# A third of four gate quarters computed in its PSUM bank, with a new pacing table, in a spectral mixing and gated feed-forward kernel

## The chip, the cores and the metric

The kernel runs on one core of a Trainium2 chip. The metric is the device time of one execution in microseconds. The kernel before took 1727.75 us (median of three runs, 1726.9 to 1728.06).

A core has five instruction streams that run side by side and meet at semaphores: TensorE (PE, with weight loads listed apart as PEld), VectorE (DVE), ScalarE (ACT), GpSimd (POOL) and SyncE (SP), which here only issues DMA transfers. Matrix products end in PSUM, which this kernel uses as eight banks of 128 x 512 float32. Each stream executes its instructions in the order in which the program lists them.

## The reference

The input `x` has 8192 tokens of 448 channels. Two functions of it are multiplied and added to it:

```
xn  = layernorm(x)
s   = irfft( softshrink( W2 . relu( W1 . rfft(xn) + b1 ) + b2 ) )   # along the 8192 tokens; W1, W2 complex,
                                                                    # block-diagonal, 4 blocks of 112
g   = silu( (gelu(xn @ w_gate) * (xn @ w_up)) @ w_down )            # hidden width 1792
out = x + s * g
```

So `s` is a Fourier filter over the tokens and `g` a gated feed-forward layer, token by token.

## The kernel before

**Precision.** Every matrix product is made of float16 parts. A float32 operand is split into a high and a low half, and three products (high by high, high by low, low by high) are added in PSUM. Large products are moreover cut into 2 x 2 blocks and made with seven block products in place of eight (`PROD`, `PROD2`). That leaves many sums and splits of float32 tiles for VectorE, ScalarE and GpSimd.

**Two passes of the feed-forward part.** The 8192 tokens are cut into 16 chunks of 512. The hidden width is cut into 14 tiles of 128: pass one (`p == 0`) handles eight tiles for all chunks and writes each chunk's partial down-projection to DRAM (`prt`); pass two (`p == 1`) handles the other six tiles and adds the partial. A chunk (`chunk`) is a series of units of two hidden tiles (`unit`). A unit makes its products 1, 5, 6, 4, 2, 3, 7 into one bank of the ring `bx` and two banks of the ring `by`; each ring has two banks. Product 1 goes into the `bx` bank `X`; a ScalarE copy (`seed`, seen in the trace as `by<-bx`) takes it to a `by` bank `Z`; product 5 takes the other `by` bank; product 6 (`a6`) adds to `X` and waits for that copy.

**The down-projection** of a chunk (`down2`) makes four quarters, each 128 x 448 (two token columns by half the channels). The first one, `QS[0]`, is built partly in a `bd` bank and partly in a `by` bank `z`; the second in the `bd` bank that serves on for a later quarter; the last two in `bd` banks. Half of this work stands at the end of the chunk, the other half (`tail`) is taken into the first unit of the next chunk.

**The gate of a quarter in pass two** (`ended2`, lines 1811 to 1864). With `u` half the down-projection, `silu(2u) = u (1 + tanh u)`. Three instructions compute it: scale the bank and add the partial loaded from `prt` (VectorE), tanh (ScalarE), `(tanh + 1) * u` (VectorE). The partial lies in one of four SBUF slots (`PT`, seen in the trace as the tile `left`, since the slots lie in that tile's space); SP loads a new partial as soon as a slot is free. For the last two quarters the sum `u` is written back into the bank itself, the slot is free after the first instruction and the bank after the third. For the first two the sum goes to the slot: the bank is free after the first instruction and the slot after the third. The result `th` is then stored to DRAM (`gsp`) for the first eleven chunks, and for the later ones multiplied with `s` at once.

**The Fourier part** runs between these. Phase 1 (until about 645 us) normalizes `x` and does a first transform; phase 2 (until about 1470 us) does the second transform, the block products, softshrink and the first inverse transform in 64 groups; phase 3 does the last inverse transform, multiplies by the gate, adds `x` and stores.

**What sets the order.** The program is written by a planner, the class `Pace`. Each piece of work is a Python generator; `Pace.run` advances them in the order of planned times and so writes one order for each engine. Planned times come from a cost for every instruction (`cost`), the planned end of what it reads (`ready`), and rings that hand out a bank or slot when its last use is planned to be over (`Ring`, `Slots`). The planner's settings change with planned time by the table `STEPS`, whose entries are a time and five numbers: an allowance for each DMA transfer's landing, the backlog at which an engine counts as busy (not in force after phase 1, where a constant 1.8 us is larger), a factor on every cost but TensorE's, a bias in choosing GpSimd over VectorE, and a factor on the distance between the starts of Fourier chunks, groups or tiles. `Either` picks VectorE or GpSimd for sums of SBUF tiles.

Of the kernel before, what the change touches and what calls it, by code (L numbers as in the profile page):

```python
# [22 lines left out]
NG = 16  # L23
# [16 lines left out]
GROUPS = tuple((j, min(4, 64 - j)) for j in range(1, 64, 4))  # L40
POS = (0, 2, 1, 3)
EPS = 1e-5
STEPS = ((0, 2.75, 0.05, 1.0, 0.0, 1.0), (15, 2.75, 0.05, 1.0, 0.0, 1.0), (25, 2.75, 0.05, 0.96, 0.2, 1.0), (35, 2.75, 0.05, 0.96, 0.2, 1.0), (45, 2.75, 0.05, 1.08, 0.1, 1.0), (55, 2.75, 0.05, 1.08, 0.1, 1.0), (65, 2.75, 0.05, 1.07, 0.0, 1.0), (75, 2.75, 0.05, 1.07, 0.0, 1.0), (87, 2.75, 0.15, 0.98, -0.1, 1.0), (100, 2.75, 0.15, 0.98, -0.1, 1.0), (125, 2.5, 0.15, 1.04, 0.0, 1.0), (150, 2.5, 0.15, 1.04, 0.0, 1.0), (175, 2.5, 0.15, 1.04, 0.2, 1.0), (200, 2.5, 0.15, 1.04, 0.2, 1.0), (225, 3.0, 0.15, 1.08, -0.2, 1.0), (250, 3.0, 0.15, 1.08, -0.2, 1.0), (275, 3.0, 0.15, 1.08, -0.2, 1.0), (300, 3.0, 0.15, 1.08, -0.2, 1.0), (325, 3.0, 0.05, 1.03, -0.2, 1.0), (350, 3.0, 0.05, 1.03, -0.2, 1.0), (375, 3.0, 0.05, 1.03, -0.2, 0.9), (400, 3.0, 0.05, 1.03, -0.2, 0.9), (425, 2.5, 0.15, 1.04, -0.5, 1.06), (450, 2.5, 0.15, 1.04, -0.5, 1.06), (475, 2.5, 0.1, 1.04, 0.0, 1.0), (500, 2.5, 0.1, 1.04, 0.0, 1.0), (525, 2.5, 0.1, 1.04, -0.3, 1.0), (550, 2.5, 0.1, 1.04, -0.3, 1.0), (575, 2.5, 0.1, 1.04, -0.2, 0.94), (600, 2.5, 0.1, 1.04, -0.2, 0.94), (625, 2.5, 0.1, 1.06, -0.2, 0.94), (650, 2.5, 0.1, 1.06, -0.2, 0.94), (675, 2.5, 0.1, 1.03, -0.2, 0.94), (700, 2.5, 0.1, 1.03, -0.2, 0.94), (725, 2.5, 0.1, 1.03, -0.3, 0.94), (750, 2.5, 0.1, 1.03, -0.3, 0.94), (775, 3.0, 0.05, 1.04, -0.5, 1.0), (800, 3.0, 0.05, 1.04, -0.5, 1.0), (825, 2.5, 0.05, 1.02, -0.5, 1.0), (850, 2.5, 0.05, 1.02, -0.5, 1.0), (875, 2.5, 0.05, 1.05, -0.5, 1.0), (900, 2.5, 0.05, 1.05, -0.5, 1.0), (925, 2.5, 0.05, 1.05, -0.5, 0.94), (950, 2.5, 0.05, 1.05, -0.5, 0.94), (975, 2.5, 0.05, 1.05, -0.5, 0.94), (1000, 2.5, 0.05, 1.05, -0.5, 0.94), (1025, 4.0, 0.05, 1.05, -0.5, 0.9), (1050, 4.0, 0.05, 1.05, -0.5, 0.9), (1075, 4.0, 0.05, 1.05, -0.5, 0.75), (1100, 4.0, 0.05, 1.05, -0.5, 0.75), (1125, 2.75, 0.05, 1.04, 0.0, 0.94), (1150, 2.75, 0.05, 1.04, 0.0, 0.94), (1175, 1.75, 0.05, 1.075, 0.0, 1.0), (1200, 1.75, 0.05, 1.075, 0.0, 1.0), (1225, 1.75, 0.05, 1.045, -0.5, 0.94), (1250, 1.75, 0.05, 1.045, -0.5, 0.94), (1275, 1.75, 0.05, 1.055, -0.5, 1.0), (1300, 1.75, 0.05, 1.055, -0.5, 1.0), (1325, 1.25, 0.05, 0.995, -0.5, 1.03), (1350, 1.25, 0.05, 0.995, -0.5, 1.03), (1375, 1.25, 0.05, 0.995, -0.5, 0.93), (1400, 1.25, 0.05, 0.995, -0.5, 0.93), (1425, 1.25, 0.05, 0.995, -0.5, 0.93), (1450, 1.25, 0.05, 0.995, -0.5, 0.93), (1475, 1.25, 0.05, 1.025, -0.5, 1.0), (1500, 1.25, 0.05, 1.025, -0.5, 1.0), (1525, 1.25, 0.05, 1.025, -0.5, 1.0), (1550, 1.25, 0.05, 1.025, -0.5, 1.0), (1575, 1.25, 0.05, 1.055, -0.5, 1.06), (1600, 1.25, 0.05, 1.055, -0.5, 1.06), (1625, 1.25, 0.05, 1.055, -0.5, 1.06), (1650, 1.25, 0.05, 1.055, -0.5, 1.06), (1675, 1.25, 0.1, 1.045, -0.5, 1.06), (1700, 1.25, 0.1, 1.045, -0.5, 1.06), (1725, 2.75, 0.05, 0.94, 0.4, 1.0))
QUIET = 200.0
AHEAD = 0.0
FREE = 1.8
# [12 lines left out]
class Pace:  # L59
# [498 lines left out]
def afno_geglu_kernel(ctx, tc, x, gu, raw, wd, mlp, b1, b2, c_m, c_mt, c_small, c_rows, out):  # L558
# [1106 lines left out]
    def add2(p, i, q, bank_):  # L1665

        v = part(bank_, 128, 2, DH)
        if p == 0 and ("ptb", 0, i, q) not in EV:
            t = yield from TH.get()
            EV["ptb", 0, i, q] = t, t.rearrange("p (a d) -> p a d", a=2)  # L1670
            S.activation(EV["ptb", 0, i, q][1], v, AF.Copy, scale=cB[0])
            yield
            return
        if p == 0:
            t = EV["ptb", 0, i, q][1]
        else:
            yield ev("pt", i, q)
            t = EV["ptb", i, q]
        V.scalar_tensor_tensor(t, v, cB[p], t, op0=ALU.mult, op1=ALU.add)
        yield  # L1680

    def down2(p, i, h, last):
# [1169 lines left out]
```

## Time and profile before

| | |
|---|---|
| time, median of three runs | 1727.75 us |
| the profiled execution, its own time | 1729.31 us |
| its span, first to last instruction | 1727.2 us |
| granted TensorE clock, mean | 0.998 |
| busy: PE, DVE, ACT, POOL | 1709.1, 1345.0, 1103.3, 1014.2 us |
| DMA | 316.62 MB, 183 GB/s |

Nearly all instructions are issued through a helper at line 290, so the profile is read by tiles, written as out<-in. `by<-bx` is an instruction that reads a bank of the ring `bx` and writes one of `by`. The names of interest are `bx`, `by` and `bd` (PSUM banks), `left` (also the slots of partials), `th` (the gate), `ms` (where the scale lies), `zs`, `z`, `wn`, `va`, `u` (Fourier phase 2), `g`, `mt` (phase 3), `h` and `wt` (the hidden values; `wt` also has weights and scratch).

### The profile page before, as it was taken

The page shows a single profiled execution, that of the slowest core. Times are in us where ns is not written, and L with a number is a line of the kernel's source. Part 1 is how long each engine was busy: PE and PEld are TensorE (multiplying, and loading weights), DVE is VectorE, ACT ScalarE, POOL GpSimd, SP SyncE. Part 2 cuts the span into 40 slices and gives each one's busy share as a digit, 9 for nine tenths or more (in the row PEclk, how much of TensorE's full clock was granted, in tenths as well). Part 3 has the DMA queues.
Part 4 walks back from the last instruction along what each step waited for, and adds up shares of the span by engine and source line. Part 5 has one row for each costly group of instructions (what it writes and reads, how often), then busy time and mean ns, then how long its engine had stood idle before and what let it go on. Part 6 is the DMA issues. An engine that isn't in the chain of part 4 may idle for free.

```text
span 1727.2 us, 41012 instructions
## 1 busy us (share of the span) xinstructions
PE 1709.1 (99%) x15654; PEld 1435.5 (83%) x15654; DVE 1345.0 (78%) x2317; ACT 1103.3 (64%) x2242; POOL 1014.2 (59%) x1410
## 2 busy tenths in 40 slices
PE   9999999999999999999999999999999999999998
PEld 4447677766777999998999999999999999889886
DVE  8998888778777878778786777787776786577776
ACT  6767766676756657678676667777676665333333
POOL 2487656677735785456374466654555654555556
PEclk9999999999999999999999999999999999999999
DMA  7348986997756753253535875454645544999996
GB/s 275 119 154 256 276 237 207 265 281 202 231 163 189 208 135 77 60 128 88 131 91 172 214 174 122 123 135 109 156 123 137 120 105 123 280 321 314 296 306 229
DMA packets 438308, 316.62 MB, mean 183 GB/s; under 512 B 305792, under 2 KB 409600, under 8 KB 436320
## 3 DMA queue, kind: packets, MB, share of 16 engines
q1 hardware_dynamic: 437824, 313.99, 64.4%
q8 instruction: 122, 2.00, 0.5%
q14 instruction: 74, 0.61, 0.1%
q10 hardware_dynamic: 288, 0.03, 0.0%
HBM read 137.93 MB, written 108.25 MB: 143 GB/s over the span
## 4 chain that ended last, share of the span: by engine, by line
PE 87%; DVE 6%; ACT 2%; DMA 2%; POOL 2%; issue 1%; SPq 0%; POOLq 0%; DVEq 0%; ACTq 0%
PE bd L290 35%; PE bx L290 30%; PE by L290 22%; DMA prt<-th 1%; DVE st L290 1%; ACT wt L290 1%; DVE raws L290 0%; POOL st L290 0%; DVE ysb L290 0%; DVE wt L290 0%; DVE dw L290 0%; DVE left L290 0%; DVE u L290 0%; DMA xta<-xts 0%; DVE h L290 0%
## 5 line engine op out<-in xcount | busy, mean ns | idle before, releaser
L290 PEld LDWEIGHTS <-wt 128*128 128x128 f16 x9142 | 885.4, 98 | 160.2 <-issue 8.2
L290 PE MATMUL bx<-xta,wt 128*128 128x256 f16 (+1 forms) x2819 | 354.0, 275 | 3.5 <-ACT by L290 2.6
L290 PEld LDWEIGHTS <-h 128*128 128x128 f16 x2711 | 259.8, 98 | 75.5 <-POOL h L290 1.6
L290 PE MATMUL by<-xtb,wt 128*128 128x256 f16 x2080 | 255.2, 273 | 0.4 <-DVE by L290 0.3
L290 PE MATMUL bd<-dw,h 128*128 128x448 f16 (+1 forms) x1536 | 243.1, 306 | 1.0 <-DVE ysb L290 0.7
L290 POOL TENSOR_TENSOR wt<-wt 128x256 f32<-128x256 f32 x181 | 140.2, 775 | 94.0 <-DVE wt L290 84.7
L290 PE MATMUL bx<-xtb,wt 128*128 128x256 f16 x1248 | 154.3, 274 | 2.2 <-DVE v L290 2.2
L290 PE MATMUL by<-xta,wt 128*128 128x256 f16 (+1 forms) x899 | 123.8, 282 | 0.1
L290 POOL TENSOR_TENSOR h<-wt,h 128x512 f16<-128x512 f32 (+1 forms) x92 | 96.1, 1058 | 35.9 <-ACT h L290 35.4
L290 DVE TENSOR_TENSOR by<-bx,u 128x512 f32<-128x512 f32 x104 | 72.4, 696 | 52.9 <-PE bx L290 44.9
L290 ACT ACTIVATE u<-by,fc 128x512 f32<-128x512 f32 (+1 forms) x118 | 73.6, 636 | 51.5 <-PE by L290 49.4
L290 PE MATMUL bx<-left,wt 128*128 128x256 f16 x816 | 99.9, 272 | 0.0
L290 DVE TENSOR_TENSOR v<-bx,u 128x512 f32<-128x512 f32 x104 | 71.4, 686 | 36.1 <-PE bx L290 35.5
L290 PE MATMUL bd<-dw,wt 128*128 128x224 f16 (+1 forms) x816 | 97.6, 264 | 0.5 <-DVE left L290 0.5
L290 POOL CAST zs<-t 112x256 f16<-112x256 f32 (+2 forms) x45 | 21.3, 474 | 123.1 <-DVE t L290 107.9
L290 ACT COPY u<-by 128x512 f32<-128x512 f32 x104 | 60.8, 585 | 50.2 <-PE by L290 49.4
L290 ACT CAST h<-wt 128x512 f16<-128x512 f32 (+1 forms) x128 | 68.5, 536 | 31.4 <-DVE wt L290 25.1
L290 PE MATMUL bd<-w2t,wn 113*128 113x112 f16 (+1 forms) x1152 | 77.6, 212 | 0.0
L290 ACT COPY by<-bx 128x512 f32<-128x512 f32 x104 | 59.8, 575 | 21.1 <-PE bx L290 20.8
L290 PE MATMUL bd<-wt,h 128*128 128x224 f16 x603 | 72.0, 259 | 0.8 <-POOL h L290 0.8
L290 PEld LDWEIGHTS <-wn 113*128 113x128 f16 (+1 forms) x1152 | 69.1, 97 | 2.1
L290 DVE SCALAR_TENSOR_TENSOR u<-by,fc,u 128x512 f32<-128x512 f32 (+1 forms) x86 | 55.2, 656 | 18.7 <-PE by L290 12.9
(283 smaller groups left out, 3764.8 us busy)
## 6 DMA issues: line engine op xcount, KB each, us to landing
xts<-sx SPq DMA_DIRECT2D x32, 480.0 KB, 3.6
x<-in_x SPq DMA_DIRECT2D x17, 896.0 KB, 6.2
t<-ysb SPq DMA_DIRECT2D x64, 224.0 KB, 3.8
prt<-th SPq DMA_DIRECT2D x64, 224.0 KB, 3.2
vt<-va SPq DMA_DIRECT2D x256, 56.0 KB, 2.1
left<-prt SPq DMA_DIRECT2D x64, 224.0 KB, 3.7
u<-t SPq DMA_DIRECT2D x32, 448.0 KB, 6.0
x<-in_x SPq DMA_DIRECT2D x32, 448.0 KB, 6.6
```

The lines of the kernel that those rows point to most:

```text
L290: return self.pace.issue(self.name, kind, out, ins, lambda: fn(out, *args, **kw))
```

## The change

Two edits. In `ended2`, the branch that computes the gate in the bank is taken by every quarter that is handed a bank to give back, and no more only by those with a `bd` bank; the bank goes back to its own ring. In pass two that adds the first quarter, whose bank is the `by` bank `z`, in the chunks 0 to 14. The second quarter is handed no bank and stays as it was. The second edit replaces 38 of the 75 entries of `STEPS`.

```diff
-        if R is BD and p == 1 and i < NG - 1:
+        if R and p == 1 and i < NG - 1:
             v, q = part(b, 128, 2, DH), EV["ptb", i, qq]
             V.scalar_tensor_tensor(v, v, cB[1], q, op0=ALU.mult, op1=ALU.add)
             PT.put(q)
...
             S.activation(th, v, AF.Tanh)
             yield
             V.scalar_tensor_tensor(th, th, 1.0, v, op0=ALU.add, op1=ALU.mult)
-            BD.put(b)
+            R.put(b)
             yield
             yield from gated(i, qq, tf, th)
             return
```

The changed entries of `STEPS`, neighbours with one setting taken together, as (from, to) of planned time and the five numbers:

```
 325- 375   3.0  0.05 1.03  -0.2 1.0    ->  3.0  0.05 1.03   0.0 1.0
 625- 675   2.5  0.1  1.06  -0.2 0.94   ->  2.5  0.1  1.06  -0.5 0.88
 675- 725   2.5  0.1  1.03  -0.2 0.94   ->  3.25 0.1  1.06  -0.5 0.94
 725- 775   2.5  0.1  1.03  -0.3 0.94   ->  3.25 0.1  1.06  -0.5 0.94
 775- 825   3.0  0.05 1.04  -0.5 1.0    ->  3.25 0.1  1.06  -0.5 0.94
 825- 875   2.5  0.05 1.02  -0.5 1.0    ->  3.25 0.1  1.06  -0.5 0.94
 875- 925   2.5  0.05 1.05  -0.5 1.0    ->  2.5  0.05 1.05  -0.5 0.94
 925- 975   2.5  0.05 1.05  -0.5 0.94   ->  2.5  0.05 1.01  -0.5 0.94
1075-1125   4.0  0.05 1.05  -0.5 0.75   ->  4.0  0.05 1.05  -0.5 0.9
1125-1175   2.75 0.05 1.04   0.0 0.94   ->  4.0  0.05 1.05  -0.5 0.9
1175-1225   1.75 0.05 1.075  0.0 1.0    ->  1.75 0.05 1.075 -0.3 1.0
1225-1275   1.75 0.05 1.045 -0.5 0.94   ->  1.75 0.05 1.075 -0.3 1.0
1325-1375   1.25 0.05 0.995 -0.5 1.03   ->  2.0  0.05 1.045 -0.5 1.0
1375-1475   1.25 0.05 0.995 -0.5 0.93   ->  2.0  0.05 1.045 -0.5 0.9
1525-1575   1.25 0.05 1.025 -0.5 1.0    ->  1    0.05 1.025 -0.5 1.0
1575-1625   1.25 0.05 1.055 -0.5 1.06   ->  1    0.05 1.025 -0.5 1.0
1625-1675   1.25 0.05 1.055 -0.5 1.06   ->  1.25 0.05 1.035 -0.5 1.06
1675-1725   1.25 0.1  1.045 -0.5 1.06   ->  1.25 0.05 1.075 -0.5 1.06
```

The entries before 325 us and the remaining ones are as they were.

More of the change, by code (lines that the diff above doesn't have):

```diff
@@ L42 @@
 EPS = 1e-5
-STEPS = ((0, 2.75, 0.05, 1.0, 0.0, 1.0), (15, 2.75, 0.05, 1.0, 0.0, 1.0), (25, 2.75, 0.05, 0.96, 0.2, 1.0), (35, 2.75, 0.05, 0.96, 0.2, 1.0), (45, 2.75, 0.05, 1.08, 0.1, 1.0), (55, 2.75, 0.05, 1.08, 0.1, 1.0), (65, 2.75, 0.05, 1.07, 0.0, 1.0), (75, 2.75, 0.05, 1.07, 0.0, 1.0), (87, 2.75, 0.15, 0.98, -0.1, 1.0), (100, 2.75, 0.15, 0.98, -0.1, 1.0), (125, 2.5, 0.15, 1.04, 0.0, 1.0), (150, 2.5, 0.15, 1.04, 0.0, 1.0), (175, 2.5, 0.15, 1.04, 0.2, 1.0), (200, 2.5, 0.15, 1.04, 0.2, 1.0), (225, 3.0, 0.15, 1.08, -0.2, 1.0), (250, 3.0, 0.15, 1.08, -0.2, 1.0), (275, 3.0, 0.15, 1.08, -0.2, 1.0), (300, 3.0, 0.15, 1.08, -0.2, 1.0), (325, 3.0, 0.05, 1.03, -0.2, 1.0), (350, 3.0, 0.05, 1.03, -0.2, 1.0), (375, 3.0, 0.05, 1.03, -0.2, 0.9), (400, 3.0, 0.05, 1.03, -0.2, 0.9), (425, 2.5, 0.15, 1.04, -0.5, 1.06), (450, 2.5, 0.15, 1.04, -0.5, 1.06), (475, 2.5, 0.1, 1.04, 0.0, 1.0), (500, 2.5, 0.1, 1.04, 0.0, 1.0), (525, 2.5, 0.1, 1.04, -0.3, 1.0), (550, 2.5, 0.1, 1.04, -0.3, 1.0), (575, 2.5, 0.1, 1.04, -0.2, 0.94), (600, 2.5, 0.1, 1.04, -0.2, 0.94), (625, 2.5, 0.1, 1.06, -0.2, 0.94), (650, 2.5, 0.1, 1.06, -0.2, 0.94), (675, 2.5, 0.1, 1.03, -0.2, 0.94), (700, 2.5, 0.1, 1.03, -0.2, 0.94), (725, 2.5, 0.1, 1.03, -0.3, 0.94), (750, 2.5, 0.1, 1.03, -0.3, 0.94), (775, 3.0, 0.05, 1.04, -0.5, 1.0), (800, 3.0, 0.05, 1.04, -0.5, 1.0), (825, 2.5, 0.05, 1.02, -0.5, 1.0), (850, 2.5, 0.05, 1.02, -0.5, 1.0), (875, 2.5, 0.05, 1.05, -0.5, 1.0), (900, 2.5, 0.05, 1.05, -0.5, 1.0), (925, 2.5, 0.05, 1.05, -0.5, 0.94), (950, 2.5, 0.05, 1.05, -0.5, 0.94), (975, 2.5, 0.05, 1.05, -0.5, 0.94), (1000, 2.5, 0.05, 1.05, -0.5, 0.94), (1025, 4.0, 0.05, 1.05, -0.5, 0.9), (1050, 4.0, 0.05, 1.05, -0.5, 0.9), (1075, 4.0, 0.05, 1.05, -0.5, 0.75), (1100, 4.0, 0.05, 1.05, -0.5, 0.75), (1125, 2.75, 0.05, 1.04, 0.0, 0.94), (1150, 2.75, 0.05, 1.04, 0.0, 0.94), (1175, 1.75, 0.05, 1.075, 0.0, 1.0), (1200, 1.75, 0.05, 1.075, 0.0, 1.0), (1225, 1.75, 0.05, 1.045, -0.5, 0.94), (1250, 1.75, 0.05, 1.045, -0.5, 0.94), (1275, 1.75, 0.05, 1.055, -0.5, 1.0), (1300, 1.75, 0.05, 1.055, -0.5, 1.0), (1325, 1.25, 0.05, 0.995, -0.5, 1.03), (1350, 1.25, 0.05, 0.995, -0.5, 1.03), (1375, 1.25, 0.05, 0.995, -0.5, 0.93), (1400, 1.25, 0.05, 0.995, -0.5, 0.93), (1425, 1.25, 0.05, 0.995, -0.5, 0.93), (1450, 1.25, 0.05, 0.995, -0.5, 0.93), (1475, 1.25, 0.05, 1.025, -0.5, 1.0), (1500, 1.25, 0.05, 1.025, -0.5, 1.0), (1525, 1.25, 0.05, 1.025, -0.5, 1.0), (1550, 1.25, 0.05, 1.025, -0.5, 1.0), (1575, 1.25, 0.05, 1.055, -0.5, 1.06), (1600, 1.25, 0.05, 1.055, -0.5, 1.06), (1625, 1.25, 0.05, 1.055, -0.5, 1.06), (1650, 1.25, 0.05, 1.055, -0.5, 1.06), (1675, 1.25, 0.1, 1.045, -0.5, 1.06), (1700, 1.25, 0.1, 1.045, -0.5, 1.06), (1725, 2.75, 0.05, 0.94, 0.4, 1.0))
@@ new lines @@
+STEPS = ((0, 2.75, 0.05, 1.0, 0.0, 1.0), (15, 2.75, 0.05, 1.0, 0.0, 1.0), (25, 2.75, 0.05, 0.96, 0.2, 1.0), (35, 2.75, 0.05, 0.96, 0.2, 1.0), (45, 2.75, 0.05, 1.08, 0.1, 1.0), (55, 2.75, 0.05, 1.08, 0.1, 1.0), (65, 2.75, 0.05, 1.07, 0.0, 1.0), (75, 2.75, 0.05, 1.07, 0.0, 1.0), (87, 2.75, 0.15, 0.98, -0.1, 1.0), (100, 2.75, 0.15, 0.98, -0.1, 1.0), (125, 2.5, 0.15, 1.04, 0.0, 1.0), (150, 2.5, 0.15, 1.04, 0.0, 1.0), (175, 2.5, 0.15, 1.04, 0.2, 1.0), (200, 2.5, 0.15, 1.04, 0.2, 1.0), (225, 3.0, 0.15, 1.08, -0.2, 1.0), (250, 3.0, 0.15, 1.08, -0.2, 1.0), (275, 3.0, 0.15, 1.08, -0.2, 1.0), (300, 3.0, 0.15, 1.08, -0.2, 1.0), (325, 3.0, 0.05, 1.03, 0.0, 1.0), (350, 3.0, 0.05, 1.03, 0.0, 1.0), (375, 3.0, 0.05, 1.03, -0.2, 0.9), (400, 3.0, 0.05, 1.03, -0.2, 0.9), (425, 2.5, 0.15, 1.04, -0.5, 1.06), (450, 2.5, 0.15, 1.04, -0.5, 1.06), (475, 2.5, 0.1, 1.04, 0.0, 1.0), (500, 2.5, 0.1, 1.04, 0.0, 1.0), (525, 2.5, 0.1, 1.04, -0.3, 1.0), (550, 2.5, 0.1, 1.04, -0.3, 1.0), (575, 2.5, 0.1, 1.04, -0.2, 0.94), (600, 2.5, 0.1, 1.04, -0.2, 0.94), (625, 2.5, 0.1, 1.06, -0.5, 0.88), (650, 2.5, 0.1, 1.06, -0.5, 0.88), (675, 3.25, 0.1, 1.06, -0.5, 0.94), (700, 3.25, 0.1, 1.06, -0.5, 0.94), (725, 3.25, 0.1, 1.06, -0.5, 0.94), (750, 3.25, 0.1, 1.06, -0.5, 0.94), (775, 3.25, 0.1, 1.06, -0.5, 0.94), (800, 3.25, 0.1, 1.06, -0.5, 0.94), (825, 3.25, 0.1, 1.06, -0.5, 0.94), (850, 3.25, 0.1, 1.06, -0.5, 0.94), (875, 2.5, 0.05, 1.05, -0.5, 0.94), (900, 2.5, 0.05, 1.05, -0.5, 0.94), (925, 2.5, 0.05, 1.01, -0.5, 0.94), (950, 2.5, 0.05, 1.01, -0.5, 0.94), (975, 2.5, 0.05, 1.05, -0.5, 0.94), (1000, 2.5, 0.05, 1.05, -0.5, 0.94), (1025, 4.0, 0.05, 1.05, -0.5, 0.9), (1050, 4.0, 0.05, 1.05, -0.5, 0.9), (1075, 4.0, 0.05, 1.05, -0.5, 0.9), (1100, 4.0, 0.05, 1.05, -0.5, 0.9), (1125, 4.0, 0.05, 1.05, -0.5, 0.9), (1150, 4.0, 0.05, 1.05, -0.5, 0.9), (1175, 1.75, 0.05, 1.075, -0.3, 1.0), (1200, 1.75, 0.05, 1.075, -0.3, 1.0), (1225, 1.75, 0.05, 1.075, -0.3, 1.0), (1250, 1.75, 0.05, 1.075, -0.3, 1.0), (1275, 1.75, 0.05, 1.055, -0.5, 1.0), (1300, 1.75, 0.05, 1.055, -0.5, 1.0), (1325, 2.0, 0.05, 1.045, -0.5, 1.0), (1350, 2.0, 0.05, 1.045, -0.5, 1.0), (1375, 2.0, 0.05, 1.045, -0.5, 0.9), (1400, 2.0, 0.05, 1.045, -0.5, 0.9), (1425, 2.0, 0.05, 1.045, -0.5, 0.9), (1450, 2.0, 0.05, 1.045, -0.5, 0.9), (1475, 1.25, 0.05, 1.025, -0.5, 1.0), (1500, 1.25, 0.05, 1.025, -0.5, 1.0), (1525, 1, 0.05, 1.025, -0.5, 1.0), (1550, 1, 0.05, 1.025, -0.5, 1.0), (1575, 1, 0.05, 1.025, -0.5, 1.0), (1600, 1, 0.05, 1.025, -0.5, 1.0), (1625, 1.25, 0.05, 1.035, -0.5, 1.06), (1650, 1.25, 0.05, 1.035, -0.5, 1.06), (1675, 1.25, 0.05, 1.075, -0.5, 1.06), (1700, 1.25, 0.05, 1.075, -0.5, 1.06), (1725, 2.75, 0.05, 0.94, 0.4, 1.0))
```

## The prediction

> **What bounds the kernel now.** I read the page's busy shares first, then the busy time by stretches that I cut at the stages, then TensorE's waits from 325 us on (the first planner time whose settings the diff changes).
>
> ```profile
> PE 1709.1 (99%) x15654; PEld 1435.5 (83%) x15654; DVE 1345.0 (78%) x2317; ACT 1103.3 (64%) x2242; POOL 1014.2 (59%) x1410
> ```
>
> ```profile
> 0.00:325.00 325.00, 317.11 (x2060) 199.53 (x2061) 280.40 (x533) 222.55 (x454) 196.63 (x342) 0.99 0.73 223
> 325.00:625.00 300.00, 299.15 (x2414) 235.15 (x2412) 235.61 (x437) 201.09 (x393) 201.77 (x342) 1.00 0.73 206
> 625.00:965.00 340.00, 338.94 (x3610) 314.08 (x3609) 261.60 (x457) 237.11 (x518) 193.84 (x247) 1.00 0.47 118
> 965.00:1470.00 505.00, 504.51 (x5298) 465.90 (x5296) 382.04 (x638) 345.60 (x710) 277.07 (x331) 1.00 0.54 133
> 1470.00:1700.00 230.00, 230.00 (x2114) 204.80 (x2112) 167.29 (x231) 87.10 (x153) 125.96 (x132) 1.00 0.97 303
> 1700.00:1720.70 20.70, 19.41 (x172) 16.02 (x169) 15.88 (x22) 9.20 (x16) 16.41 (x16) 1.00 0.64 223
> 1720.70:1727.20 6.50, 0.00 (x0) 0.00 (x0) 2.17 (x4) 0.68 (x2) 2.47 (x3) 0.72 0.32 106
> ```
>
> In the stretch rows the columns are: length, busy time (and count) of PE, PEld, DVE, ACT, POOL, granted clock, DMA share, GB/s. The reader is to see that TensorE is the bound and has almost nothing left to give. Its idle time is the first number less the second: 7.89 us before 325, then 0.85, 1.06, 0.49, 0.00, 1.29, and 6.50 after the last matmul, together 18.1 of 1727.2 us. Neither part of the change alters a matmul, so the 1709.1 us stay. The program up to 325 us stays as it is too, so its 7.89 us stay. The last 6.5 us are the final elementwise work and the last store, which the diff leaves alone. What is left to win is 0.85 + 1.06 + 0.49 + 1.29 = 3.69 us. TensorE's waits from 325 us to the end are few and single; the one that matters below is this (total, times, longest):
>
> ```profile
> PE bx L290 <- ACT by L290: 0.7, 1, 0.7
> ```
>
> 0.2% of the median, 1727.75 us, is 3.46 us, about what a measurement of this kernel can tell from no change. So a gain that can be told needs nearly every wait gone, while a loss has no such ceiling.
>
> **The gate itself.** Line 1817 now takes the first quarter's branch too. Fifteen chunks of the second pass (all but its last) have this quarter. Per quarter the same three instructions stay, with other places: scale-and-add into the `by` bank and no longer into the partial's slot, tanh from the bank, the second multiply with one operand in the bank. The profile has both forms, since two quarters already go this way (columns: count, busy us, mean ns, idle before).
>
> ```profile
> L290 DVE SCALAR_TENSOR_TENSOR th<-th,left 128x448 f32<-128x448 f32 x30 | 21.6, 720 | 6.9 <-ACT th L290 6.7
> ...
> L290 DVE SCALAR_TENSOR_TENSOR bd<-bd,ms,left 128x448 f32<-128x448 f32 x30 | 20.7, 691 | 12.4 <-PE bd L290 12.0
> ...
> L290 ACT ACTIVATE th<-left 128x448 f32<-128x448 f32 x33 | 19.0, 577 | 29.6 <-DVE left L290 29.6
> ...
> L290 DVE SCALAR_TENSOR_TENSOR th<-th,bd 128x448 f32<-128x448 f32 x30 | 18.4, 613 | 0.3
> ...
> L290 ACT ACTIVATE th<-bd 128x448 f32<-128x448 f32 x30 | 16.3, 544 | 20.3 <-DVE bd L290 20.3
> ...
> L290 DVE SCALAR_TENSOR_TENSOR left<-by,ms,left 128x448 f32<-128x448 f32 x16 | 10.9, 680 | 1.4 <-PE by L290 0.6
> ```
>
> First instruction 691 - 680 = +11 ns, tanh 544 - 577 = -33 ns, last 613 - 720 = -107 ns. Over 15 quarters VectorE works 15 x (0.107 - 0.011) = 1.4 us less and ScalarE 0.5 us less. Price on the path: 0. TensorE hides it: it works 504.51 of 505 and 230 of 230 us in the two stretches that hold the fifteen quarters, and VectorE only 382 and 167. Were VectorE the bound there, it would be worth -1.4 us, which I keep as the lower end.
>
> [...]
>
> The partial's slot comes free after the first instruction and no more after the last, some 577 + 720 ns = 1.3 us sooner. So the next chunk's first load of a partial may be issued by SP that much earlier. The sums read it only at that chunk's end, some 45 us on (the copies below stand at 1362 and 1409 us). Price 0.
>
> **The bank held longer.** This is the cost. Before, the `by` bank came free after the first instruction; now also tanh and the second multiply must be through. There are two `by` banks. After the quarter the next chunk's first unit takes both: one for product 5, and this one for a ScalarE copy (`by<-bx`), which product 6 into `bx` waits for. I read the timelines of the three engines at all fifteen boundaries. The worst one, VectorE first, then ScalarE, then TensorE (start, length, engine, operation):
>
> ```profile
> 1407.23 2.33 DVE L290 TENSOR_TENSOR h<-wt,h 128x512 f16<-128x512 f32 x1
> ...
> 1410.22 0.61 DVE L290 SCALAR_TENSOR_TENSOR th<-th,left 128x448 f32<-128x448 f32 x1
> ```
>
> ```profile
> 1408.81 0.57 ACT L290 COPY by<-bx 128x512 f32<-128x512 f32 x1 [0.31 <-PE bx L290]
> 1410.33 0.35 ACT L290 CAST zs<-t 112x192 f16<-112x192 f32 x1 [0.96 <-DVE t L290]
> ```
>
> ```profile
> 1410.29 1.25 PE L290 MATMUL bx<-left,wt 128*128 128x256 f16 x10
> ```
>
> The copy takes the bank at 1408.81, when the second multiply, behind a long `h<-wt,h`, has not begun. In this order the bank would be free at 1410.83, the copy over at 1410.83 + 0.57 = 1411.40, and product 6, which began at 1410.29, 1.11 us late. Behind the copy in ScalarE's order stands the cast of `zs`, for which matmuls of the Fourier stage wait in turn. Two more boundaries have the multiply after the copy's start:
>
> ```profile
> 1362.28 0.57 ACT L290 COPY by<-bx 128x512 f32<-128x512 f32 x1 [0.71 <-PE bx L290]
> ...
> 1362.91 0.61 DVE L290 SCALAR_TENSOR_TENSOR th<-th,left 128x448 f32<-128x448 f32 x1
> ...
> 1363.17 1.25 PE L290 MATMUL bx<-xta,wt 128*128 128x256 f16 x10
> ```
>
> ```profile
> 1168.38 0.57 ACT L290 COPY by<-bx 128x512 f32<-128x512 f32 x1 [0.18 <-PE bx L290]
> ...
> 1168.66 0.61 DVE L290 SCALAR_TENSOR_TENSOR th<-th,left 128x448 f32<-128x448 f32 x1
> ...
> 1169.84 1.25 PE L290 MATMUL bx<-xta,wt 128*128 128x256 f16 x10
> ```
>
> Here the delay is 1363.52 + 0.57 - 1363.17 = 0.92 us, and 1169.27 + 0.57 - 1169.84 = 0. At a fourth (the boundary at 1117 us) multiply and copy overlap, but product 6 begins late enough. At the other eleven the multiply is through before the copy starts, in the store stage by a wide margin; the last of them:
>
> ```profile
> 1664.21 0.69 DVE L290 SCALAR_TENSOR_TENSOR th<-th,left 128x448 f32<-128x448 f32 x1
> ...
> 1666.64 0.57 ACT L290 COPY by<-bx 128x512 f32<-128x512 f32 x1 [0.50 <-PE bx L290]
> ```
>
> The multiply ends at 1664.90, 1.7 us ahead. So the old order with the new rule would cost 1.11 + 0.92 = 2.0 us. But the order is written anew by a planner that knows when the bank comes free: it can put Fourier matmuls ahead of product 6, and the work so displaced costs nothing as long as there is some. Bounds: 0 to 2.0 us. The nearest row is the wait of PE for `by` from ScalarE: one of 0.7 us after 325 us, and none between 625 and 1700 us. I take 0.
>
> **The pacing table.** It moves no instruction to another unit of work; it changes the times that the planner assumes, which of VectorE and GpSimd takes an operation, and how far apart the Fourier groups start. So it can only create or remove waits. The lower bound is all 3.69 us gone. For the upper I give the whole rest the worst rate of the four stretches up to 1700 us, 1.06 per 340 us: 1375 x 0.00312 = 4.29 where now 2.40 us stand, +1.9. Between the ends I take the rate of the longest stretch, 965 to 1470 us, 0.49 per 505: 1375 x 0.00097 = 1.33 for 2.40, so -1.1 us. The 1.29 us at the end I leave.
>
> **Sum.** 0 (gate) + 0 (bank) - 1.1 (table) on the profiled execution: span 1727.2 to 1726.1, its own time 1729.31 to 1728.2. That execution stands 1.56 us above the median of 1727.75, so the time to expect is 1726.65, say **1726.7 us**.
>
> **Rivals.** *The bank locks the boundary (slower).* Place: the copy `by<-bx` at the chunk boundaries before 1470 us, of which the second pass has ten. VectorE is busiest there, and one long instruction (the 2.33 us of `h<-wt,h` above) holds the multiply back. It decides from the point where the multiply ends later than about 0.6 us before product 6 would start. Price about 1.0 us each (mean of 1.11 and 0.92); at five boundaries with nothing to fill in, 5.1 us: 1732.9; at all ten 1738. Four are enough for a loss that can be told. For it: at four of ten the multiply was late, at two with a price. Against: TensorE waited for no such copy between 625 and 1700 us. [...]
>
> *The table removes every wait (faster).* -3.69 us: 1724.1. For it: the changed entries cover every wait after 625 us, and 230 us without any idle time show that it can be done. Against: it must succeed in four stretches and make no new wait.
>
> *The store stage starts later (slower).* From 1470 to 1700 us the DMA engines are at 0.97, 223 us of work. Spare are 7 us there and 0.36 x 20.7 = 7.5 us after. If the new spacing ends the Fourier stage more than some 14 us later, stores end late; at 20 us it is 6 us: 1733.8. Against: the spacing is corrected towards a fixed end at each group.
>
> *The change does nothing.* The test `if R` is true for the bank's ring object and false only where no bank is passed, so the quarter does move.
>
> **Chances.** Forecast 0.68, own range 1725.3 to 1729.7 (table -2.4 to +1.9); every wait gone 0.15; bank 0.13; store stage 0.04. Range for 8 in 10: from all waits gone and half a microsecond of spread, 1723.6, to both upper bounds together, 1727.75 + 1.9 + 2.0 = 1731.7. Faster than 1724.3 us: 0.12, most of the second case. Slower than 1731.2: 0.15, most of the last two. Same: 0.73.
>
> **What would show it.** Right: fifteen rows `by<-by,ms,left` on VectorE with one `left<-by` left; tanh `th<-by` x15 at about 544 ns; last multiply `th<-th,by` x15 at about 613; PE busy within 1 us of 1709; idle before 325 us near 7.9. Bank wrong: waits of PE `bx` for ACT `by` between 1010 and 1450 us, the copy starting right at the multiply's end. Table wrong: idle after 325 us above 5.6 us, or below 1. Store stage: first stage-three load well after 1471 us. The prediction as a whole is wrong if PE's busy time moves by several microseconds, or the idle time before 325 us does.

## The result, and the profile after

The changed kernel takes 1734.76 us, the median of 6 runs (1733.47 to 1736.15), beside 1727.51 us for the kernel before on the same chip (6 runs). The ratio is 1.0042, 95% interval 1.003 to 1.0055: slower by 7.25 us, where 1726.7 us was forecast and 1731.7 us was the upper end of the range. The profiled execution took 1734.73 us, almost the median itself.

First the page's busy shares:

```profile
PE 1710.3 (99%) x15654; PEld 1435.8 (83%) x15654; DVE 1334.9 (77%) x2306; ACT 1100.5 (64%) x2244; POOL 1014.8 (59%) x1419
```

TensorE has the same 15,654 matmuls and 1.2 us more of work. VectorE has 10 us less of it, which is worth nothing, as it isn't the bound. So the loss is idle time of TensorE and, for a smaller part, matmuls that run slower. The same stretches as before, with the same columns (length, busy time of PE, PEld, DVE, ACT, POOL, clock, DMA share, GB/s):

```profile
0.00:325.00 325.00, 318.23 (x2081) 200.79 (x2081) 281.02 (x535) 224.99 (x458) 196.65 (x343) 1.00 0.74 226
325.00:625.00 300.00, 299.15 (x2418) 235.45 (x2416) 238.28 (x439) 199.63 (x391) 201.54 (x345) 1.00 0.73 203
625.00:965.00 340.00, 335.37 (x3565) 309.88 (x3564) 252.31 (x440) 240.58 (x525) 194.94 (x252) 0.99 0.45 113
965.00:1470.00 505.00, 503.49 (x5275) 464.90 (x5274) 375.85 (x631) 336.20 (x699) 280.38 (x334) 1.00 0.56 134
1470.00:1700.00 230.00, 230.00 (x2113) 204.79 (x2112) 165.17 (x232) 87.11 (x153) 120.09 (x126) 1.00 0.99 304
1700.00:1720.70 20.70, 18.13 (x156) 14.54 (x154) 14.65 (x20) 10.03 (x17) 16.51 (x17) 1.00 0.66 228
1720.70:1732.90 12.20, 5.97 (x60) 5.44 (x57) 7.61 (x13) 1.93 (x4) 4.66 (x5) 0.91 0.32 113
```

Length less PE busy gives the idle time, after against before:

| stretch, us | before | after | difference |
|---|---|---|---|
| 0 to 325 | 7.89 | 6.77 | -1.12 |
| 325 to 625 | 0.85 | 0.85 | 0 |
| 625 to 965 | 1.06 | 4.63 | +3.57 |
| 965 to 1470 | 0.49 | 1.51 | +1.02 |
| 1470 to 1700 | 0.00 | 0.00 | 0 |
| 1700 to the end | 7.79 | 8.80 | +1.01 |
| PE busy, whole span | 1709.1 | 1710.3 | +1.2 |

The differences sum to 5.7 us, which is the difference of the spans, 1732.9 less 1727.2. The measured difference of the medians is larger, since the profiled execution of before was one of its longer ones (1729.31 us, 1.80 above the median of six), while that of the changed kernel lies at its median. The program up to 325 us is the same in both, so the -1.12 is no effect of the change. The largest entry is the stretch from 625 to 965 us. TensorE's waits from 325 us on (total, times, longest) name what it waited for:

```profile
PE bd L290 <- DVE bd L290: 2.4, 1, 2.4
PE bd L290 <- DMA mt<-c_mt: 2.3, 2, 1.5
PE bd L290 <- DVE wn L290: 1.5, 1, 1.5
...
```

The first and the third are single waits, of 2.4 and 1.5 us, and both name VectorE. Neither has to do with the gate: they stand at 819 and 682 us, in the first pass of the FFN, while the gate edit acts in the second. The timeline around them (start, length, engine, operation; in brackets the wait before it and its releaser):

```profile
678.98 3.13 DVE L290 TENSOR_TENSOR wn<-t,wn 112x256 f16<-112x256 f32 x1
...
678.94 0.67 POOL L290 TENSOR_TENSOR left<-gl,left 128x256 f16<-128x256 f32 x1
679.57 1.16 POOL L290 TENSOR_TENSOR left<-u,left 128x512 f16<-128x512 f32 x1
680.68 1.15 POOL L290 TENSOR_TENSOR h<-u,h 128x512 f16<-128x512 f32 x1
...
682.17 0.67 PE L290 MATMUL bd<-w2t,wn 112*128 112x112 f16 x10 [1.51 <-DVE wn L290]
...
815.27 3.55 DVE L290 TENSOR_TENSOR zs<-t,zs 112x256 f16<-112x256 f32 x1
...
814.82 0.72 POOL L290 TENSOR_TENSOR u<-u 128x256 f32<-128x256 f32 x1
815.51 0.67 POOL L290 TENSOR_TENSOR h<-gl,h 128x256 f16<-128x256 f32 x1
816.13 0.67 POOL L290 TENSOR_TENSOR left<-gl,left 128x256 f16<-128x256 f32 x1
816.76 0.67 POOL L290 TENSOR_TENSOR h<-gl,h 128x256 f16<-128x256 f32 x1
817.39 1.15 POOL L290 TENSOR_TENSOR left<-u,left 128x512 f16<-128x512 f32 x1
...
818.75 0.39 DVE L290 TENSOR_TENSOR bd<-bd,o 128x224 f32<-128x224 f32 x1
...
819.19 0.54 PE L290 MATMUL bd<-w2t,wn 113*128 113x112 f16 x6 [2.40 <-DVE bd L290]
819.51 2.45 PE L290 MATMUL bd<-dw,h 128*128 128x224 f16 x12
821.75 1.27 PE L290 MATMUL by<-dw,h 128*128 128x224 f16 x6
```

Two VectorE instructions take 3.13 and 3.55 us. The timeline of the kernel before has the second one at its usual length, and one that is lengthened in the same way:

```profile
680.79 2.94 DVE L290 TENSOR_TENSOR left<-gl,left 128x256 f16<-128x256 f32 x1
...
683.99 0.41 DVE L290 TENSOR_TENSOR zs<-t,zs 112x256 f16<-112x256 f32 x1
```

Each of the two ends 0.28 us after the last of an unbroken row of GpSimd instructions that was under way when it began: 682.11 us after 681.83, and 818.82 after 818.54. TensorE needs their results, or those of the instruction queued behind, and stands still. After the second wait the matmuls themselves are slow: twelve of 128x224 take 2.45 us and six take 1.27, where the same two groups take 1.31 and 0.74 us in e4 (last section). That is 1.67 us more, and the clock of 0.99 in that stretch. PE busy over the whole span rises by less, 1.2 us; the profiled execution of before has slow matmuls of its own before 325 us: its clock is 0.50 from 156.79 to 160.20 us, and twelve of 128x256 take 2.54 us at 156.58, where twelve take 1.47 at 161.74. From 325 us on, idle time and slow matmuls together are 3.57 + 1.02 + 1.01 + 1.67 = 7.27 us, close to the 7.25 measured.

This gave the theory to be tested: the gate edit costs nothing, as forecast; the loss is in the order that the planner wrote anew. The new order has places where GpSimd runs several instructions on end while VectorE stands at one that waits for the whole row.

### The profile page after: what moved, and what is told of

Read it like the earlier page. It is cut to its first block, busy times and chain, and to the rows that moved or that the text cites. A ratio compares the mean times of both kernels' runs of the same rounds, so it can differ in the third digit from the quotient of the medians.

```text
span 1732.9 us, 41038 instructions
## 1 busy us (share of the span) xinstructions
PE 1710.3 (99%) x15654; PEld 1435.8 (83%) x15654; DVE 1334.9 (77%) x2306; ACT 1100.5 (64%) x2244; POOL 1014.8 (59%) x1419
## 4 chain that ended last, share of the span: by engine, by line
PE 86%; DVE 6%; ACT 2%; POOL 2%; issue 2%; DMA 1%; SPq 0%; DVEq 0%; ACTq 0%; POOLq 0%
PE bd L290 35%; PE bx L290 29%; PE by L290 22%; DMA prt<-th 1%; DVE wt L290 1%; POOL wt L290 1%; DVE h L290 1%; DVE wn L290 0%; DVE u L290 0%; DVE wst L290 0%; ACT h L290 0%; DMA raws<-in_gu 0%; POOL h L290 0%; ACT wt L290 0%; POOL st L290 0%
## 5 line engine op out<-in xcount | busy, mean ns | idle before, releaser
L290 POOL TENSOR_TENSOR wt<-wt 128x256 f32<-128x256 f32 x186 | 143.7, 772 | 101.9 <-DVE wt L290 91.6
L290 POOL TENSOR_TENSOR h<-wt,h 128x512 f16<-128x512 f32 (+1 forms) x89 | 91.4, 1040 | 59.8 <-ACT h L290 59.5
L290 PEld LDWEIGHTS <-w1t 112*112 112x112 f16 x612 | 66.2, 130 | 2.6 <-issue 0.7
```

Source lines behind the costliest of these rows:

```text
L290: return self.pace.issue(self.name, kind, out, ins, lambda: fn(out, *args, **kw))
```

## The experiments

All ratios are to the kernel before, timed beside each kernel on the same chip.

| kernel | gate | table or order | us | ratio, 95% interval |
|---|---|---|---|---|
| changed kernel | bank | new | 1734.76 | 1.0042, 1.003 to 1.0055 |
| e1_gate_old_table | bank | old | 1732.92 | 1.0033, 1.002 to 1.0045 |
| e2_table_old_gate | slot | new | 1741.7 | 1.0083, 1.0069 to 1.0096 |
| e3_gate_new_table_from_975 | bank | new from 975 on | 1730.7 | 1.0021, 1.0012 to 1.003 |
| e4_old_gate_new_table_to_975 | slot | new before 975 | 1740.96 | 1.0076, 1.0064 to 1.0089 |
| e5_gate_in_old_order | bank, 11 chunks | every order as before | 1727.48 | 0.9997, 0.9988 to 1.0006 |
| e6_old_gate_nudge_975 | slot | one number moved | 1731.85 | 1.0022, 1.0013 to 1.003 |
| e7_old_gate_nudge_1025 | slot | one number moved | 1739.02 | 1.0062, 1.005 to 1.0075 |
| e8_rows_cleared | bank | as changed, 7 GpSimd operations replaced | 1729.43 | 1.001, 1.0001 to 1.0019 |
| e9_rows_opened | bank, 11 chunks | as before, 4 tiny copies more | 1726.12 | 0.9988, 0.9979 to 0.9997 |
| e10_after_rows_opened | bank | as changed, 2 tiny copies more | 1731.64 | 1.002, 1.0011 to 1.0029 |

### The two edits apart

The first has the gate edit and the old table, the second the new table and the old gate.

```diff
-        if R is BD and p == 1 and i < NG - 1:
+        if R and p == 1 and i < NG - 1:
...
-            BD.put(b)
+            R.put(b)
```

> The gate edit alone, with the pacing table of before. Theory A (the new table's entries from 625 to 975 us make the loss: in the changed kernel's trace TensorE stands 1.5 us at 682 us and 2.4 us at 819 us, before the first edited quarter at 1015 us, each time behind a VectorE instruction that took over 3 us beside a row of GpSimd instructions): 1726 to 1730 us, no such wait before 975 us, everything before about 966 us as in the kernel before. Theory B (the bank held longer makes it): 1732 us or more, with waits of PE bx for ACT by between 1015 and 1470 us. Theory C (neither: every new order draws its own waits): anywhere from 1726 to 1734, with new waits after 1015 us on various instructions.

```diff
-STEPS = (the old 75 entries)
+STEPS = (the new 75 entries)
```

> The new table alone, with the gate of before. Theory A: 1732 to 1736 us, with the waits at 682 and 819 us in their places, since the program up to 966 us is that of the changed kernel. Theory B: 1726 to 1729 us. Theory C: the waits before 966 us stay (about 5.5 us more than before), those after are drawn anew, 1731 to 1737 us.

The gate alone costs 5.6 us (1732.92 less the 1727.33 of before, timed beside it), the table alone some 14, above all three ranges expected. Were these prices of the edits, both together would cost about 20; they cost 7.25. So neither number is the price of an edit. What the two kernels share is that in both the order was written anew. The first has new waits between 965 and 1470 us on several instructions (1.5 us for `v`, 1.4 for `zs`, 1.3 for the copy into `by`), as theory C has it. The one place where the bank itself is late in the first (ScalarE's copy and the product 6 that waits for it, with the gate's last multiply on VectorE):

```profile
1218.27 0.61 DVE L290 SCALAR_TENSOR_TENSOR th<-th,by 128x448 f32<-128x448 f32 x1
```

```profile
1220.20 0.60 ACT L290 COPY by<-bx 128x512 f32<-128x512 f32 x1
```

```profile
1220.85 1.25 PE L290 MATMUL bx<-left,wt 128*128 128x256 f16 x10 [1.30 <-ACT by L290]
```

The multiply ended at 1218.88, the copy began 1.3 us later. So the bank was free by then; the copy was late because of its place in ScalarE's order, behind three other instructions. That the planner put it there because it books the bank for longer is argued, not shown. Price 1.3 us, at one boundary.

### The table cut at 975 us

```diff
-STEPS = (the new 75 entries)
+STEPS = (the old entries before 975, the new ones from 975 on)
```

> The gate edit with the new table's entries from 975 us on, the old ones before. Theory A: 1727 to 1730 us, without the waits at 682 and 819 us; what the later entries add (the changed kernel's trace has some 2 us more of TensorE waits from 975 us to the end) may stay. Theory B: 1732 us or more. Theory C: 1726 to 1734.

```diff
-STEPS = (the old 75 entries)
+STEPS = (the new entries before 975, the old ones from 975 on)
```

> The gate of before, the new entries of the table up to 975 us, the old ones after. Theory A: 1731 to 1734 us, the waits at 682 and 819 us in their places, about 5.5 us above the kernel before. Theory B: 1726 to 1729 us. Theory C: 1731 to 1737, the waits before 975 us in place and others after.

Without the new entries before 975 the changed kernel takes 1730.7 us, which is 3.4 us above the kernel before where it was 7.25 with them; that is 0.7 above theory A's range and inside theory C's. With those entries alone the old gate takes 1740.96, again above all three ranges expected. Both long VectorE instructions of the changed kernel come with them, and e4 has the wait of 2.4 us too. But e4 also has 6.6 us of idle time between 965 and 1470 us, with the old entries there, where the kernel before has 0.49:

```profile
965.00:1470.00 505.00, 498.40 (x5207) 458.38 (x5206) 382.08 (x637) 335.72 (x691) 269.70 (x325) 1.00 0.56 133
```

So new entries early in the table shift what follows them as well. That the changed kernel lost less than e2 and e4 is luck of its order as far as is known.

### The gate with the order held still

Here the planner books the three instructions with their old operands, so that it writes the old order; what is emitted computes in the bank. This was done in the eleven chunks (0, 1, 4 to 6, 9 to 14) where the old order gives the bank back in time.

```diff
+        if R is BY and p == 1 and i in KEEP:
+            yield ev("pt", i, qq)
+            v, q = part(b, 128, 2, DH), EV["ptb", i, qq]
+            pace.issue("DVE", "scalar_tensor_tensor", q, [v, cB[1], q], lambda: nc.vector.scalar_tensor_tensor(
+                v, v, cB[1], q, op0=ALU.mult, op1=ALU.add))
...
+            pace.issue("ACT", "activation", th, [q], lambda: nc.scalar.activation(th, v, AF.Tanh))
...
+            pace.issue("DVE", "scalar_tensor_tensor", th, [th, q], lambda: nc.vector.scalar_tensor_tensor(
+                th, th, 1.0, v, op0=ALU.add, op1=ALU.mult))
```

> The table of before, and the gate computed in the bank in the eleven chunks (0, 1, 4, 5, 6 and 9 to 14) whose last multiply stood before the copy into the bank; the planner still books the old instructions, so every engine's order is that of the kernel before and only the operands of 33 instructions differ. Theory 'order' (the edit itself costs nothing, what costs is that the planner writes another order): 1726.5 to 1728 us, no new wait of TensorE over 0.5 us. Theory 'bank' (holding the bank costs of itself): 1729 us or more, waits of PE bx for ACT by at the boundaries near 1018, 1219 and 1455 us, where the multiply had ended only 0.0 to 0.15 us before the copy.

The order of every engine is that of before, 33 instructions have other operands, and the time is 1727.48 against 1727.98 us, ratio 0.9997. From 325 us on TensorE's waits are those of before; among them are

```profile
PE bx L290 <- DVE v L290: 0.7, 1, 0.7
PE bd L290 <- DVE left L290: 0.5, 1, 0.5
PE bd L290 <- DVE zs L290: 0.3, 1, 0.3
```

So the gate in the bank costs nothing that can be told in these eleven chunks (interval 0.9988 to 1.0006); four weren't tried in this way.

### One number of the old table moved

The old gate, the old table, and one entry changed: the cost factor at 975 us from 1.05 to 1.06, or the distance factor at 1025 us from 0.9 to 0.91.

```diff
-(975, 2.5, 0.05, 1.05, -0.5, 0.94)
+(975, 2.5, 0.05, 1.06, -0.5, 0.94)
```

> The kernel before with one number of the table changed: the cost factor of the entry at 975 us, 1.05 to 1.06. The same work, the order from there on written anew. Theory 'order': 1730 to 1737 us, some 3 to 10 us of new waits after 975 us, on VectorE results that come late. Theory 'bank' or any theory that puts the loss on the edit: 1726.5 to 1729.

```diff
-(1025, 4.0, 0.05, 1.05, -0.5, 0.9)
+(1025, 4.0, 0.05, 1.05, -0.5, 0.91)
```

> The kernel before with another single number changed: the group distance factor of the entry at 1025 us, 0.9 to 0.91. Theory 'order': 1730 to 1737 us, waits at other places than in the run with the first number changed. Theories that put the loss on the edit: 1726.5 to 1729.

They cost 3.9 and 11.0 us, the second more than the 1737 us expected at most. A change that means nothing costs as much as the change under study or more. The timeline of the first one shows the same pattern as above, once more:

```profile
1008.28 3.68 DVE L290 TENSOR_TENSOR wt<-wt,wt 128x512 f16<-128x512 f32 x1
```

```profile
1010.25 1.17 POOL L290 TENSOR_TENSOR wt<-wt,wt 128x512 f16<-128x512 f32 x1
```

```profile
1015.03 1.31 PE L290 MATMUL bd<-dw,wt 128*128 128x224 f16 x12 [1.23 <-DVE left L290]
```

VectorE's instruction stands until 1011.96 us, GpSimd's row ends at 1011.42; what VectorE had queued behind is late, and TensorE waits 1.23 us. This is read from the timeline alone; the row wasn't taken away here. Not every new wait is of this kind: the longest of the second, 4.35 us at 1214.93 for `t`, has no lengthened instruction right before it, and its cause was not followed up.

### The rows taken away

The changed kernel, with its order kept; the seven GpSimd subtractions of the two rows at 679 and 815 us are each replaced by a memset of the same tile. This leaves a part of the computation out: the low halves of the hidden values that these seven produce are zero.

```diff
+            if self.name == "POOL" and op == "tensor_sub":
+                CLEAR.append(0)
+                if len(CLEAR) - 1 in ROWS:
+                    return self.pace.issue(self.name, kind, out, ins, lambda: self.engine.memset(out, 0.0))
```

> The changed kernel with every engine's order kept, but seven GpSimd subtractions (the three that run from 679 to 682 us, the four from 815.5 to 818.5 us) replaced by a memset of the same tile, so that GpSimd reads nothing from SBUF there; the low halves of those h and left tiles are left out as zeros. Theory 'lock-out' (a VectorE instruction with two SBUF inputs stands still until a row of GpSimd instructions that read SBUF is through): wn<-t,wn and zs<-t,zs, 3.13 and 3.55 us in the changed kernel, take 0.4 to 0.7 us, the waits of 1.5 us at 682 and 2.4 us at 819 us go, the 18 slow matmuls after 819 us too: 1729 us, 5 to 6 us less than the changed kernel. Rival (those VectorE instructions are late for another reason, or other waits take the place): 1733 us or more.

The time is 1729.43 us, 5.3 less than the changed kernel's (1.45 above the kernel before, timed beside it, where that was 7.25 above). The profiled execution was the longest of its eleven (1734.67 us), so only its stretch and its rows are read:

```profile
625.00:965.00 340.00, 339.27 (x3630) 314.70 (x3629) 251.42 (x448) 243.84 (x532) 196.51 (x261) 1.00 0.46 118
```

```profile
682.78 0.41 DVE L294 TENSOR_TENSOR wn<-t,wn 112x256 f16<-112x256 f32 x1
```

```profile
817.40 0.55 DVE L294 TENSOR_TENSOR zs<-t,zs 112x256 f16<-112x256 f32 x1
```

Idle time in the stretch is 0.73 us where it was 4.63; the two instructions take 0.41 and 0.55 us, and the clock is 1.00. But a memset is also shorter than a subtraction (the four of the second row take 0.32, 0.32, 0.32 and 0.53 us where the subtractions took 0.67, 0.67, 0.67 and 1.15), so this alone doesn't tell the row from the amount of work.

### The rows opened

Two kernels with all their work. A GpSimd copy of 64 partitions by one element is put into a row; it reads the result of the VectorE instruction that stands still there, so GpSimd must let that one through first (it waits 0.34 us for it at both rows of the changed kernel). It writes to an element that GpSimd's next instruction overwrites.

```diff
+def opened(eng, out):
+    k = CALLS[eng.name] = CALLS.get(eng.name, -1) + 1
+    if eng.name == "DVE" and k in OPEN.values():
+        OUT[k] = out
+    if eng.name == "POOL" and k in OPEN:
+        eng.engine.tensor_copy(corner(out), corner(OUT[OPEN[k]]))
...
-            return self.pace.issue(self.name, kind, out, ins, lambda: fn(out, *args, **kw))
+            return self.pace.issue(self.name, kind, out, ins, lambda: opened(self, out) or fn(out, *args, **kw))
```

In the changed kernel, at its two rows:

> The changed kernel with its own order and all of its work, and two tiny GpSimd copies (64 partitions x 1 element): one after the second instruction of the row at 679 us, which reads the result of wn<-t,wn (3.13 us there), one at the head of the row at 815 us, which reads the result of zs<-t,zs (3.55 us there). If the rows hold the VectorE instructions back, both fall below 1.2 us, the TensorE waits of 1.51 us at 682 and 2.40 us at 819 and the slow matmuls after the second go away, and the time is about 1729.3 us as with the cleared rows, ratio 1.001 to the kernel before. If clearing the rows helped for another reason (less GpSimd work), the time stays near 1734.8, ratio 1.004. If GpSimd's wait makes its own results late, new waits on POOL show behind the two places and the time lies between.

```profile
682.39 0.18 POOL L2865 COPY left<-wn 64x1 f16<-64x1 f16 x1 [0.34 <-DVE wn L290]
...
817.67 0.18 POOL L2865 COPY h<-zs 64x1 f16<-64x1 f16 x1 [0.34 <-DVE zs L290]
```

```profile
681.42 0.90 DVE L290 TENSOR_TENSOR wn<-t,wn 112x256 f16<-112x256 f32 x1
...
817.04 0.56 DVE L290 TENSOR_TENSOR zs<-t,zs 112x256 f16<-112x256 f32 x1
```

```profile
PE bd L290 <- DVE bd L290: 0.8, 1, 0.8
...
```

The two instructions fall from 3.13 and 3.55 us to 0.90 and 0.56, and of TensorE's waits in the stretch from 625 to 965 us (the last fence) the 2.4 and 1.5 are gone. The matmuls after 819 us take 1.31 and 0.74 us again. No work was taken away here, so it is the row that held the two instructions. A new wait of 0.8 us stands at 687: the rest of the first row now runs on beside later VectorE instructions, and those take longer there (`gl<-v,fc,gl` 1.51 us and `o<-h` 1.17, where the changed kernel has 0.74 and 0.21). The time is 1731.64 us: 3.1 of the 5.4 us expected. It lies between, as in the third of the three cases, but the new wait names VectorE and not GpSimd, and what keeps the other 2.3 us isn't shown.

In the order of before, at four rows of its own (one wait of 0.3 us near 684, one of 0.7 near 799, one of 0.5 near 1065, shown with e5 above):

> The order of the kernel before (with the gate in the bank in eleven chunks, which was measured at no change), and four tiny GpSimd copies (64 partitions x 1 element) put into four of its rows of GpSimd instructions: each reads the result of the VectorE instruction that stands still during that row, so that GpSimd has to let it through first. Nothing is left out of the computation. If a VectorE instruction with two SBUF inputs is held until the whole row of GpSimd instructions is through, the three TensorE waits that the trace of the kernel before shows behind such instructions (0.3 us near 684, 0.7 near 799, 0.5 near 1065) go away, and the time is 1726.0 us, 1.5 below the kernel before, ratio 0.9991. If GpSimd's own wait costs as much as it frees, or the long VectorE times have another cause, the time stays at 1727.5 to 1728.0, ratio 1.000, with the three waits still there or moved.

```profile
...
PE by L290 <- DVE by L290: 0.6, 1, 0.6
PE bd L290 <- DMA vt<-va: 0.4, 1, 0.4
...
```

```profile
625.00:965.00 340.00, 340.00 (x3623) 314.99 (x3621) 257.57 (x457) 238.05 (x521) 192.81 (x247) 1.00 0.47 118
```

All three waits are gone, TensorE has no idle time left between 625 and 965 us, and of the gain some is spent on a new wait of 0.4 us for a DMA. The 0.6 for `by` lies between 325 and 625 us, where nothing had been put in. The time is 1726.12 us, against 1727.8 us of before beside it: 0.9988, 0.9979 to 0.9997. It is 1.7 us below the kernel before, where 1.5 was expected. This is the fastest kernel of the study, with the gate in the bank in eleven chunks. As the gate alone gave 0.9997, the gain is put down to the copies; the two intervals overlap, so it rests on the three waits that went more than on the time.

## Why the prediction was wrong

**The gate itself, price 0: right.** The three forms came out as costed (columns: count, busy us, mean ns, idle before).

```profile
L290 DVE SCALAR_TENSOR_TENSOR by<-by,ms,left 128x448 f32<-128x448 f32 x15 | 10.3, 685 | 0.6
...
L290 DVE SCALAR_TENSOR_TENSOR th<-th,by 128x448 f32<-128x448 f32 x15 | 9.2, 616 | 3.1 <-ACT th L290 2.9
...
L290 ACT ACTIVATE th<-by 128x448 f32<-128x448 f32 x15 | 8.1, 543 | 9.7 <-DVE by L290 9.5
```

685, 543 and 616 ns where 691, 544 and 613 were taken from the `bd` quarters; and e5 shows the price on the path, nothing that can be told. The last multiply takes 616 ns with the bank, and took 720 without it in the kernel before. But 720 is a mean that a few long ones draw up: the thirty run from 606 to 1230 ns with a median of 624. So most of the 107 ns a quarter that I took for the place of the operand isn't that.

**The bank held longer, price 0, bounds 0 to 2.0: right in size.** In the changed kernel one boundary of the fifteen has a wait for the copy into the bank, of 0.28 us:

```profile
1367.98 1.25 PE L290 MATMUL bx<-xta,wt 128*128 128x256 f16 x10 [0.28 <-ACT by L290]
```

The rival of the locked boundary, 1.0 us each at five or more, fell. What it missed is where the price would come from: the copy is late by its place in the order, the bank being free (1.30 us in e1; here the multiply ends at 1366.35 and the copy begins at 1367.34).

**The order written anew, booked under the pacing table at -1.1 us, bounds -3.69 to +1.9: wrong, and nearly the whole of the miss.** The measured loss is 7.25 us. About 5.2 of it stand in the stretch from 625 to 965 us (3.57 of idle time and 1.67 of slow matmuls), 1.0 in the next, 1.0 at the end. Without the new entries before 975 the loss is 3.4. The mechanism that I gave, "it can only create or remove waits", held as far as it goes. Three steps failed. The upper bound: "For the upper I give the whole rest the worst rate of the four stretches" takes the waits of one order as the worst that an order can have. The matmuls: "Neither part of the change alters a matmul, so the 1709.1 us stay" gave no price to matmuls that run slower after a wait, 1.67 us. And the redraw was booked under the table alone: of the gate edit I wrote that the work displaced "costs nothing as long as there is some", but with the old table it costs 5.6 us in e1, of which the bank's boundary is at most 1.3. The order of before was an unusually good one for its surroundings: every order that was written anew in this study, by the gate, by the table, by either half of the table or by one number, was slower, by 3.4 to 14 us. A bound for a rewritten order has to come from orders other than the one at hand, and no row of before gives it. But one row of before did show the cause at a smaller price: `left<-gl,left`, 2.94 us at 680.79, with TensorE's wait of 0.3 us behind it near 684. I quoted a 2.33 us `h<-wt,h` myself and used it for the bank alone.

**"Every wait gone", 1724.1 us: fell.** Idle time after 325 us rose from 2.40 to 6.99 by 1700 us.

**"The store stage starts later": not in that form.** TensorE is busy for the whole of 1470 to 1700 us, as before. The first load of that stage (`u<-t`) comes 6.0 us later (1477.60 for 1471.60), well inside the 14 us of slack that I gave it, and yet TensorE waits 2.3 us for two loads of `mt` after 1700 us, where before it had no such wait; idle time from 1700 us to the end is 1.0 us more. That the later start makes these waits isn't shown: in e8 and e10 the stage starts more than 2 us sooner (1475.15 and 1475.34), and the waits for `mt` are 3.5 and 3.0 us.

**What would show it.** "Idle after 325 us above 5.6 us", apart from the final 6.2, was named as the sign that the table is wrong: it is 0.85 + 4.63 + 1.51 + 2.57 = 9.56. PE's busy time was to lie within 1 us of 1709 and is 1710.3; the slow matmuls alone are 1.67. The first 325 us were to be idle near 7.9 and are 6.8; e5, with the program of before there, has 7.4.

**Still open:** why these redraws cost between 3.4 and 14 us and which part of each is due to rows of GpSimd; in the changed kernel, the 2.0 us after 965. Only the two rows of the changed kernel and the four places of before were tested by taking the cause away.

## What to carry to other kernels

Where the bound engine is busy for 99% of the span and the order is written by a planner, an edit's own price and the price of the order that follows from it are two questions: hold the order still to measure the first, and for the second expect a loss where the present order has few waits left; their sum doesn't bound it. Look in the timeline for VectorE instructions that take several times their usual length, and see whether they end with a row of GpSimd instructions. If they do, a tiny GpSimd instruction that depends on the held one can be put into the row: in the changed kernel the two held ones fell so from 3.13 and 3.55 us to 0.90 and 0.56. Four such instructions took three waits out of the old order, and two took 3.1 us off the changed one, but brought a new wait of 0.8 us.

## What the runs showed of the hardware

**In the changed kernel two rows of GpSimd instructions held a VectorE instruction until the row was through.** A VectorE instruction with two inputs in SBUF (`zs<-t,zs`), 0.41 us long in the kernel before at 683.99 us, took 3.55 us beside a row of GpSimd instructions without a gap, 0.55 when the last four were memsets (e8), and 0.56 when GpSimd had to wait for it ahead of these four (e10). What I had not expected is that VectorE waited through several instructions: through three at 679 us, in 3.13 us, and through the rest of one and four more at 815, in 3.55. It isn't always so. Elsewhere in the same trace VectorE is let in between two GpSimd instructions that follow each other without a gap:

```profile
949.74 0.92 DVE L290 TENSOR_TENSOR h<-gl,h 128x256 f16<-128x256 f32 x1
...
949.71 0.67 POOL L290 TENSOR_TENSOR h<-gl,h 128x256 f16<-128x256 f32 x1
950.34 0.85 POOL L290 TENSOR_TENSOR left<-gl,left 128x256 f16<-128x256 f32 x1
```

VectorE's instruction ends at 950.66, 0.28 us after GpSimd's first, and GpSimd's second takes 0.85 us where the median of its twenty in this trace is 0.67. What decides between the two is open; a row is worth breaking only where the trace shows VectorE held to its end.

**In two of three kernels a gap of 2.4 us on TensorE was followed by slow matmuls.** After the wait at 819 us of the changed kernel twelve matmuls take 2.45 us and six more 1.27. In e4 the same wait, with the same matmuls behind it, has none of it:

```profile
818.90 0.46 PE L290 MATMUL bd<-w2t,wn 113*128 113x112 f16 x6 [2.39 <-DVE bd L290]
819.20 1.31 PE L290 MATMUL bd<-dw,h 128*128 128x224 f16 x12
820.35 0.74 PE L290 MATMUL by<-dw,h 128*128 128x224 f16 x6
```

In e2, as in the changed kernel, the twelve take 2.45 us, after a wait of 2.40. In the changed kernel that is 2.45 + 1.27 us against 1.31 + 0.74, 1.67 us for the eighteen. The granted clock there (columns as above):

```profile
819.43:822.84 3.41, 3.41 (x23) 2.82 (x21) 2.63 (x6) 2.86 (x5) 0.86 (x1) 0.50 1.08 214
```

It is 0.50 for these 3.41 us, and 1.00 in the 3.41 us before them, which hold the gap, and in the 3.41 us after. Over the stretch from 625 to 965 us it is 0.99 in the changed kernel and in e2, and 1.00 in e4. So a wait of 2.40 us was followed by slow matmuls in two kernels, and one of 2.39 us was not in the third. What sets e4 apart isn't shown; no run moved the gap to test it.
